# Top-32 attention and an ELU feed-forward on one core: the last queries of two batches as a block of their own, and two query tiles taken one by one

## The chip, the cores and the metric

The kernel runs on one core of a Trainium2 chip. A core has five engines that work side by side, each on its own queue of instructions in a fixed order: TensorE (PE, matrix products and transposes), VectorE (DVE), ScalarE (ACT), GpSimd (POOL) and SyncE (SP, which issues transfers). They wait for each other through semaphores. The metric is the device time of one execution in microseconds (us); the time before is the median of three runs, 1645.8 us (1644.03 to 1645.95).

## The reference

Eight batches of eight heads, 576 queries and keys of 64 numbers each; then a feed-forward of width 2048 over the 4608 tokens of 512 numbers. The weights arrive as 64-bit floats, all arithmetic of the kernel is fp32.

```python
scores = scale * np.matmul(q, k.transpose(0, 1, 3, 2))
kth = np.partition(scores, -top_k, axis=-1)[..., -top_k:-top_k + 1]   # top_k = 32
scores = np.where(scores >= kth, scores, -1000000000.0)
attn = np.exp(scores - np.max(scores, axis=-1, keepdims=True))
attn = attn / (np.sum(attn, axis=-1, keepdims=True) + 1e-09)
attn_out = np.matmul(attn, v)
x = attn_out.transpose(0, 2, 1, 3).reshape(B * S, H * D)              # 4608 x 512
h = x @ w_in                                                          # 512 x 2048
g = np.where(h > 0.0, h, np.exp(np.minimum(h, 0.0)) - 1.0)
out = g @ w_out                                                       # 2048 x 512
```

## The kernel before

**Attention.** The queries of a batch are cut into four tiles of 128 (qt 0 to 3) and a rest of 64 (qt 4, called J). A `Step` is one query tile with one pair of heads (`hp`), or the rest with four heads; a batch has 4 x 4 + 2 = 18 steps, and the program 144. In a step PE computes the scores (`scores`, L331, out tile scps) and ACT copies them out (L339); DVE finds the 32 largest of each row with MAX8 and MATCH_REPLACE8 (`select`, L373 to L385); ACT masks and exponentiates (`mask`, L407, L408); POOL normalises (`normalise`, L418 to L425); PE transposes the probabilities (`turn`, L444, eps) and ACT copies them to et (L445). When all tiles of a `Group` have been turned, PE multiplies with v (`attend`, L470, avps), for all its tiles at once, and ACT writes the result to the transposed input xT of a block (`finish`, L497).

**Order.** From step `tight` = 8 on, the order of every engine is the order in which the program is written. Program step n issues the scores of step n+2, the attend of the groups that are complete, DVE's selection for step n, the mask of step n-1, and the transposes of step n-2. The steps of an even batch run through the tiles (0, 1), (2, 3), J, those of an odd batch through J, (0, 1), (2, 3); within a pair of tiles the two alternate, head pair by head pair, and share a group. Only in batch 0 the four tiles go one by one. The k and q of later batches are loaded some steps ahead by SP and transposed by DVE (`transpose_qk`, L285, kqT); there are five kqT buffers for the four head pairs of a batch.

**Feed-forward.** Queries that go through the feed-forward together are a `Block`, of one to three slots of 128 tokens. Batches are planned in twos: the list `division` (L605, L607) names the tiles of each block, 0 to 3 for the even batch, 4 to 7 for the odd one, and `rest` for one slot that holds the 64 last queries of both. When all tiles of a block are there, `finish` appends the block's pieces to a list `ffn`: 16 pieces `hidden(f)`, each four products into hps (L545) with 128 columns to a slot, the ELU on ACT (L555 to L564) and its last sum, a "gate", on POOL (L515), or on DVE (L517) early and for the last block; then for each slot four pieces `project`, each four products into ops (L573) with 512 columns. Pieces are taken from the front of the list only. An fp32 product is two instructions on PE.

**Pace.** The function `feed` is called four times in a step and takes pieces while a running allowance holds. Every piece has a planned cost: HIDDEN[slots] for a hidden piece, PROJECT for a project piece (L21, L22), in planned us. Every block has a place `ready`, in steps, at which it will be complete; `due` lists it with the sum of the costs of all blocks ahead of it. The allowance grows by the smallest, over the blocks still to come, of the work ahead of the block divided by the steps left until it is ready. What is left after the last step is issued at the end without pause (`while ffn`).

T (L104) is the number of tokens of the widest block; it sizes the tiles of xT, gT and n. A block of one slot takes its xT from a pool of three (`xpool`), a wider one from a pool of two. The weights are decoded from 64-bit floats in the first steps (L176 to L193); pieces wait until their weights are there (`decoded`).

Of the kernel before, what the change touches and what calls it, by code (L numbers as in the profile page):

```python
# [17 lines left out]
TAKEN = -1.0e30  # L18
EPS = 1.0e-9
STEEP = 2.0**96  # L20
HIDDEN = {1: 1.1, 2: 1.85, 3: 2.7}  # L21
PROJECT = 3.55  # L22


# [57 lines left out]
def kernel(  # L82
# [10 lines left out]
    P = nc.NUM_PARTITIONS  # L93
# [7 lines left out]
    NC = dm // P  # L101
    NF = dff // P
    NG = NF // 2
    T = 3 * P  # L104
    KEYS, QUERIES = R, R + S
    Q = 32
    NB = S // Q
# [383 lines left out]
    def finish(blk, parts, at, cols, src):  # L491
        if blk.xT is None:
            if blk.slots == 1:
                blk.xT = xpool.tile([P, NC, P], FP32, tag="xT", name="xT")
            else:
                blk.xT = late["x"].tile([P, NC, T], FP32, tag="xT", name="xT")
        nc.scalar.copy(blk.xT[:, at, cols], src)  # L497
# [23 lines left out]
    def ffn_pieces(blk):  # L521
# [4 lines left out]
        def hidden(f):  # L526
# [3 lines left out]
            elif f % NG == 0 and blk.number > 0:  # L530
                g = late["g"].tile([P, NG, T], FP32, tag="g", name="gT")
                blk.gT.append(g[:])
            if f % unit == 0:
# [4 lines left out]
                else:  # L538
                    n = late["f"].tile([P, 2 * T], FP32, tag="n", name="n")
                blk.n = n[:, 0 : unit * n_tok].rearrange("p (f t) -> p f t", f=unit)  # L540
# [45 lines left out]

        part = HIDDEN[blk.slots]
        behind = 2 * NF if blk.number else 0
# [13 lines left out]
    for b in range(B):  # L602
        if b % 2 == 0:
            rest = 2 * J
            division = [(0,), (1,), (2,), (3,), (rest,), (4, 5), (6, 7)]  # L605
            if b > 0:
                division = [(0, 1), (2, 3), (rest, 4, 5), (6, 7)]  # L607
            slots = {}
            for part in division:
                blk = Block(len(blocks), len(part))  # L610
                blocks.append(blk)
                slots.update((x, (blk, s)) for s, x in enumerate(part))
        first[b] = len(steps)
        tiles = []
        for qt in range(J + 1):
            r0 = b * S + (JP if qt == J else qt if b == 0 else qt * P)
            if qt == J:
                (blk, slot), c0, n = slots[rest], (b % 2) * R, R
                rows = slice(r0, r0 + R)
            else:  # L620
                (blk, slot), c0, n = slots[(b % 2) * J + qt], 0, P
                rows = slice(r0, r0 + J * (P - 1) + 1, J) if b == 0 else slice(r0, r0 + P)
            c0 += slot * P
            t = Tile(b, qt, rows, blk, slice(c0, c0 + n))
            blk.left += NHP
            blk.tiles[slot].append(t)
            tiles.append(t)
        order = [(0, 1), (2, 3), (J,)] if b % 2 == 0 else [(J,), (0, 1), (2, 3)]
        if b == 0:
            order[:2] = [(0,), (1,), (2,), (3,)]  # L630
        for qts in order:
            for hp in range(NHP // 2 if qts == (J,) else NHP):
                group = Group([tiles[qt] for qt in qts], hp)
                steps += [Step(tiles[qt], hp, group, i) for i, qt in enumerate(qts)]
            for qt in qts:
                n = len(steps)
                tiles[qt].block.ready = n + 1.0 if n <= tight else n + 2.5
    NS = len(steps)
    total = 0.0
    for blk in sorted(blocks, key=lambda x: x.ready):  # L640
        due.append((blk.ready, total))
        total += NF * HIDDEN[blk.slots] + 4 * blk.slots * PROJECT

# [57 lines left out]
    main, rest, other = slice(0, J), slice(J, J + 1), slice(J + 1, 2 * J + 1)  # L701
# [90 lines left out]
```

## Time and profile before

| | |
|---|---|
| median of three runs | 1645.8 us |
| the profiled execution | 1642.57 us, its span 1640.8 us |
| busy: PE, DVE, ACT, POOL | 1581.7, 1453.4, 1187.7, 708.7 us |
| hps products, L545 | 1408 instructions of 256 columns, 640 of 128, 384 of 384 |
| ops products, L573 | 1152 instructions of 512 columns |
| avps products, L470 | 1120 of 256 columns, 320 of 128, 640 of 64 |
| DVE's selection, L373 to L385 | 136 steps of 8 MAX8 and 6 MATCH_REPLACE8, about 0.75 us each |
| last selection of DVE ends at | 1520 us |

An instruction of PE starts before the one ahead of it has ended, and the ends in the profile are modelled. So the price of a group of matmuls is best read from start to start: from the start of the first to the start of what follows. A step of DVE is read from one L373 to the next but one (a step has two, shown as one line where they follow each other). The granted clock of PE is 0.5 to 0.9 of full speed in the first 164 us, and 0.98 to 1.00 after.

### The profile page before, as it was taken

The page shows a single profiled execution, that of the slowest core. Times are in us where ns is not written, and L with a number is a line of the kernel's source. Part 1 is how long each engine was busy: PE and PEld are TensorE (multiplying, and loading weights), DVE is VectorE, ACT ScalarE, POOL GpSimd, SP SyncE. Part 2 cuts the span into 40 slices and gives each one's busy share as a digit, 9 for nine tenths or more (in the row PEclk, how much of TensorE's full clock was granted, in tenths as well). Part 3 has the DMA queues.
Part 4 walks back from the last instruction along what each step waited for, and adds up shares of the span by engine and source line. Part 5 has one row for each costly group of instructions (what it writes and reads, how often), then busy time and mean ns, then how long its engine had stood idle before and what let it go on. Part 6 is the DMA issues. An engine that isn't in the chain of part 4 may idle for free.

```text
span 1640.8 us, 25344 instructions
## 1 busy us (share of the span) xinstructions
PE 1581.7 (96%) x8276; PEld 1011.8 (62%) x8276; DVE 1453.4 (89%) x2981; ACT 1187.7 (72%) x2400; POOL 708.7 (43%) x1534
## 2 busy tenths in 40 slices
PE   4788999999999999999999999999999999999999
PEld 3566777666575757555566666655557575755564
DVE  6987999999999999999999699999999599998000
ACT  6887778778695867778678686868759595958521
POOL 4775445445353534445335353535435353534300
PEclk8579999999999999999999999999999999999999
DMA  7431221012100310012100211012100201000000
GB/s 226 151 128 25 50 40 26 7 22 45 42 1 7 59 42 8 7 22 44 36 14 15 43 30 28 1 28 44 36 14 0 43 1 35 1 13 2 7 13 14
DMA packets 188037, 56.18 MB, mean 34 GB/s; under 512 B 178177, under 2 KB 179201, under 8 KB 187905
## 3 DMA queue, kind: packets, MB, share of 16 engines
q1 hardware_dynamic: 186704, 54.26, 14.1%
q8 instruction: 66, 1.08, 0.3%
q14 instruction: 67, 0.54, 0.1%
q10 hardware_dynamic: 1200, 0.30, 0.1%
HBM read 45.09 MB, written 9.44 MB: 33 GB/s over the span
## 4 chain that ended last, share of the span: by engine, by line
PE 76%; ACT 12%; DVE 7%; POOL 3%; issue 1%; DMA 1%; SPq 0%; ACTq 0%; DVEq 0%; POOLq 0%
PE ops L573 29%; PE hps L545 23%; PE avps L470 10%; PE scps L331 7%; PE eps L444 6%; DVE wk L378 3%; DVE m L385 3%; ACT sc L408 2%; ACT et L445 2%; ACT sc L407 2%; DVE m L373 1%; ACT n L564 1%; ACT n L555 1%; ACT sc L339 1%; ACT n L560 1%
## 5 line engine op out<-in xcount | busy, mean ns | idle before, releaser
L385 DVE MAX8 m<-wk 128x8 f32<-128x576 f32 x816 | 577.9, 752 | 0.3 <-POOL den L406 0.3
L545 PE MATMUL hps<-xT,w_in 128*128 128x256 f32 (+2 forms) x2432 | 545.8, 374 | 0.0
L573 PE MATMUL ops<-w_out,gT 128*128 128x512 f32 x1152 | 523.6, 599 | 0.0
L545 PEld LDWEIGHTS hps<-xT,w_in 128*128 128x128 f32 x2432 | 406.0, 192 | 100.1 <-issue 26.3
L378 DVE MATCH_REPLACE8 wk<-m,wk 128x576 f32<-128x576 f32 x544 | 401.4, 748 | 0.0
L573 PEld LDWEIGHTS ops<-w_out,gT 128*128 128x128 f32 x1152 | 209.0, 190 | 233.9 <-issue 232.8
L418 POOL TENSOR_SCALAR dene<-den 128x2 f32<-128x2 f32 x144 | 32.9, 228 | 686.5 <-ACT sc L408 686.1
L408 ACT ACTIVATE sc<-sc,den 128x576 f32<-128x576 f32 x288 | 223.6, 776 | 65.5 <-POOL den L406 44.2
L407 ACT ACTIVATE sc<-sc,m 128x576 f32<-128x576 f32 x288 | 225.3, 782 | 10.8 <-DVE m L385 10.7
L470 PE MATMUL avps<-et,vT 128*64 128x256 f32 (+2 forms) x2080 | 207.2, 330 | 17.4 <-ACT et L445 17.2
L425 POOL TENSOR_SCALAR sc<-sc,rec 128x576 f32<-128x576 f32 x288 | 213.0, 750 | 15.0 <-POOL rec L423 0.2
L331 PE MATMUL scps<-kqT 64*128 64x288 f32 (+1 forms) x1280 | 206.0, 442 | 13.6 <-ACT kqT L307 9.1
L339 ACT ACTIVATE sc<-scps 128x576 f32<-128x576 f32 x288 | 171.8, 647 | 65.1 <-PE scps L331 65.1
L445 ACT COPY et<-eps 128x512 f32<-128x512 f32 x288 | 164.6, 571 | 73.4 <-PE eps L444 73.4
L378 DVE MATCH_REPLACE8 wk<-m,sc 128x576 f32<-128x576 f32 x272 | 200.6, 748 | 0.0
L373 DVE MAX8 m<-sc 128x8 f32<-128x576 f32 x272 | 191.6, 749 | 8.8 <-ACT sc L339 8.8
L444 PEld LDWEIGHTS eps<-ident,sc 128*128 128x128 f32 x1152 | 144.9, 144 | 87.2 <-issue 52.7
L444 PE MATMUL eps<-ident,sc 128*128 128x128 f32 x1152 | 177.1, 279 | 13.7 <-POOL sc L425 13.7
L470 PEld LDWEIGHTS avps<-et,vT 128*64 128x64 f32 x2080 | 128.5, 142 | 98.8 <-ACT et L445 31.7
L515 POOL TENSOR_TENSOR gT<-n,gT 128x512 f32<-128x512 f32 (+1 forms) x119 | 164.9, 1386 | 31.2 <-ACT n L564 31.1
L331 PEld LDWEIGHTS scps<-kqT 64*128 64x128 f32 (+1 forms) x1280 | 111.3, 182 | 89.5 <-issue 43.8
L555 ACT ACTIVATE n<-hps 128x512 f32<-128x512 f32 (+1 forms) x156 | 87.3, 559 | 56.8 <-PE hps L545 56.0
(53 smaller groups left out, 1089.6 us busy)
## 6 DMA issues: line engine op xcount, KB each, us to landing
raw<-in_moe_w_in_dram SPq DMA_DIRECT2D x16, 512.0 KB, 6.1
vT<-in_v_dram SPq DMA_DIRECT2D x64, 128.0 KB, 2.5
raw<-in_moe_w_out_dram SPq DMA_DIRECT2D x16, 512.0 KB, 3.6
out_dram<-osb SPq DMA_DIRECT2D x32, 256.0 KB, 2.1
kin<-in_k_dram SPq DMA_DIRECT2D x112, 72.0 KB, 2.5
qin<-in_q_dram SPq DMA_DIRECT2D x112, 72.0 KB, 2.6
kin<-in_k_dram SPq DMA_DIRECT2D x8, 128.0 KB, 4.5
vT<-in_v_dram SPq DMA_DIRECT2D x64, 16.0 KB, 2.2
```

Source lines behind the costliest of these rows:

```text
L331: nc.tensor.matmul(wide[i][rows, half, 0:HS], kq[part, q0 : q0 + u.t.ql], kq[part, k0 : k0 + HS], start=True, stop=True,)
L373: nc.vector.max(found[i], cur[i])
L378: nc.vector.match_replace(wk[i], found[i], cur[i], TAKEN)
L385: nc.vector.max(found[i], cur[i])
L407: nc.scalar.activation(sc, sc, AF.Prelu, scale=-1.0, bias=low, alpha=1.0 / STEEP)
L408: nc.scalar.activation(sc, sc, AF.Exp, scale=-STEEP, bias=gap, accum_out=u.den[:, i : i + 1])
L425: nc.gpsimd.tensor_scalar(u.sc[:, i, :], u.sc[:, i, :], rec[:, i : i + 1], 1.0, ALU.mult, ALU.mult)
L444: nc.tensor.transpose(ps[:, c * P : (c + 1) * P], sc[:, c0 : c0 + P], ident[:])
L445: nc.scalar.copy(g.et[:, chunks, u.at, :], ps[:, 0 : n * P].rearrange("p (c q) -> p c q", c=n),)
L470: nc.tensor.matmul(ps[i * D : (i + 1) * D, cols], vt[:, 2 * J + i if c == J else i * J + c, :], w, start=(c == 0), stop=(c == J),)
L545: nc.tensor.matmul(blk.h[:, f % bank, :], w_in[:, i, f * P : (f + 1) * P], blk.xT[:, i, 0:n_tok], start=(i == 0), stop=(i == NC - 1),)
L573: nc.tensor.matmul(blk.o[:], blk.gT[f // NG][:, f % NG, s * P : (s + 1) * P], w_out[:, f, :], start=(f == 0), stop=(f == NF - 1),)
```

## The change

The first two batches' block (4, 5) becomes two blocks, (4,) and (5,), and in batch 1 the tiles 0 and 1 (4 and 5 of the pair of batches) are taken one after the other, each with groups of its own. In the later pairs of batches the block of rest, 4, 5 becomes a block of the rest alone and a block (4, 5). No block has three slots any more; T shrinks to two slots, and the planned cost of a three-slot piece goes.

```diff
-HIDDEN = {1: 1.1, 2: 1.85, 3: 2.7}
+HIDDEN = {1: 1.1, 2: 1.85}
...
-    T = 3 * P
+    T = 2 * P
...
-            division = [(0,), (1,), (2,), (3,), (rest,), (4, 5), (6, 7)]
+            division = [(0,), (1,), (2,), (3,), (rest,), (4,), (5,), (6, 7)]
             if b > 0:
-                division = [(0, 1), (2, 3), (rest, 4, 5), (6, 7)]
+                division = [(0, 1), (2, 3), (rest,), (4, 5), (6, 7)]
...
             order[:2] = [(0,), (1,), (2,), (3,)]
+        if b == 1:
+            order[1:2] = [(0,), (1,)]
```

## The prediction

> **What bounds the kernel now.** I read the page first, then PE's timeline in three places, DVE's, the waits, and PE's order in the changed program. The page's first lines and slices:
>
> ```profile
> span 1640.8 us, 25344 instructions
> PE 1581.7 (96%) x8276; PEld 1011.8 (62%) x8276; DVE 1453.4 (89%) x2981; ACT 1187.7 (72%) x2400; POOL 708.7 (43%) x1534
> ...
> PE   4788999999999999999999999999999999999999
> ...
> DVE  6987999999999999999999699999999599998000
> ```
>
> Two engines are nearly full until slice 37; then PE works on alone. PE's busy time is modelled, so I take prices from starts. The first three lines below are early, the next five from 1119 us on, the last two end the program:
>
> ```profile
> 205.64 1.06 PE L545 MATMUL hps<-xT,w_in 128*128 128x128 f32 x8
> 206.53 0.60 PE L444 MATMUL eps<-ident,sc 128*128 128x128 f32 x4
> ...
> 411.07 3.60 PE L573 MATMUL ops<-w_out,gT 128*128 128x512 f32 x8
> ...
> 1118.92 2.75 PE L545 MATMUL hps<-xT,w_in 128*128 128x384 f32 x8
> ...
> 1128.58 0.60 PE L444 MATMUL eps<-ident,sc 128*128 128x128 f32 x4
> 1129.11 1.24 PE L331 MATMUL scps<-kqT 64*128 64x288 f32 x8
> 1130.28 0.65 PE L470 MATMUL avps<-et,vT 128*64 128x256 f32 x2
> 1131.68 2.37 PE L470 MATMUL avps<-et,vT 128*64 128x256 f32 x18 [0.76 <-ACT et L445]
> ...
> 1581.64 27.79 PE L545 MATMUL hps<-xT,w_in 128*128 128x256 f32 x128
> 1609.27 27.63 PE L573 MATMUL ops<-w_out,gT 128*128 128x512 f32 x64
> ```
>
> Eight hps matmuls of 128 columns take 206.53-205.64 = 0.89 us, 0.111 each. At 256 columns it is (1609.27-1581.64)/128 = 0.216, at 512 (ops) 27.63/64, about 0.43, at 384 I take 0.322 (eight run 2.58 us start to start). The price goes with the columns; 128 is only 4% dearer per column than 256. One fp32 product is two instructions in the trace. Attention costs PE 1.17 (scores) + 0.98 (nine transposes) + half of 2.31 (avps of two tiles) = 3.3 us a step.
>
> DVE's pace:
>
> ```profile
> 629.08 1.42 DVE L373 MAX8 m<-sc 128x8 f32<-128x576 f32 x2
> ...
> 638.71 1.42 DVE L373 MAX8 m<-sc 128x8 f32<-128x576 f32 x2
> ```
>
> A step costs DVE 9.64 us, 10.96 where a k and q pair is transposed. Now the waits:
>
> ```profile
> DVE kqT L285 <- PE scps L331: 32.3, 3, 16.9
> ```
>
> DVE loses 32 us in three places to PE's scores, not the other way round: in steps 86 and 122 PE lies 14 and 17 us behind DVE, and DVE stops till PE has caught up. So late in the kernel PE binds. Earlier it leads: it issues the scores that open step 28 at 321.3 us, when DVE starts step 28 at 329.3.
>
> From the starts of PE's scores groups I cut its time into four stretches. Work is instructions times the prices above, gap the rest:
>
> - steps 12 to 35, 170.5 to 407.0: 236.5 us, feed-forward 136.5, attention 79.4, gap 20.6 (0.86 a step)
> - steps 36 to 71, to 774.5: 367.5, feed-forward 224.6, attention 119.6, gap 23.3 (0.65 a step)
> - steps 72 to 140, to 1507.1: 732.7, feed-forward 480.1, attention 230.5, gap 22.1 (0.32 a step)
> - the end, to 1640.8: 133.7, feed-forward 114.3, attention 13.0, gap 6.4
>
> No step has a gap much below 0.2, the price of changing between kinds of matmul. The first two stretches hold some 28 us above that, where feed() rations pieces so that they last until the next block is ready. The last 55 us are the last block, which nothing can precede.
>
> **What the change does to PE's work.** In units of the planner a block of one tile costs 16 x 1.1 + 4 x 3.55 = 31.8, of two 58.0, of three 85.8. Before, the block of rest,4,5 in the second pair is ready at place 66.5 and only 391 units lie ahead of it; at step 12, with 44 done, that allows 347/54.5 = 6.4 a step, and the block (4, 5) of the first pair at 30.5 allows 6.2. After, 428 units lie ahead of 66.5 with 47 done: 7.0 a step; the tightest is 6.6 (place 38.5), then 7.1 to 7.2. After the heavy block's turn the old rate jumps to 10.7 for eight steps; that jump goes.
>
> PE's instruction order in the changed program shows this without the planner. Feed-forward work issued ahead of the scores of step 14 is 40.4 us against 37.7 (+2.7); of step 38, 180.0 against 174.2 (+5.9); of step 74, 423.3 against 398.8 (+24.5: hps 512 of 128 columns and 256 of 256, ops 232; before 320, 256, 60 of 384, and 208); of step 143, 901.1 against 878.9 (+22.2). What is left behind the last scores falls from 114.3 to 94.7.
>
> *More work.* hps products go from 320/704/192 (128/256/384 columns) to 640/832/0: 320 x 0.222 + 128 x 0.432 - 192 x 0.645 = +2.5 us. The four head pairs of the split tiles do 20 avps matmuls of 256 columns (2.31) as two of 128 (1.24 each): +0.7. Sum +3.2.
>
> The kernel's own table puts a narrow piece at 1.1 for 8 instructions, 0.137 each, which would be 640 x 0.026 = 17 us more; the trace's 0.111 stands against it. The Trainium skill ("TensorE: Matmul & The Clock Gate", section "Back-to-back issue gap") speaks against narrow pieces too: in a stream of weight loads and matmuls it gives about 81 ns at 128 columns where the isolated gap would be 56. An estimate from it, 640 further narrow instructions at 25 ns, is +16 us in place of +2.5; the row of eight in 0.89 us decides against it.
>
> *Steps 8 to 11.* Step 10 gets 2.7 us more hps. DVE closes one gate more there (0.7 us) and waits for each group in its queue, with the next MATCH_REPLACE8 behind it; it already waits 5.7 us at that place. I let everything after start 2.7 later. Bounds: 0, if DVE's wait covers it, and 5.
>
> *Steps 12 to 35.* DVE sets the pace and PE leads. PE's work grows by 3.2 + 0.7 = 3.9 in a gap of 20.6: +0. If the cover fails, +3.9; a gain is excluded, since DVE does not stop there except in step 14.
>
> *Steps 36 to 71.* DVE needs 768.0-410.4 = 357.6 us. PE's work becomes 344.2 + 18.7 = 362.9, more than DVE's: PE binds, and the waits for DVE's results go. I take the gap of the stretch that is already so, 0.32 a step: 11.5. So 374.4 against 367.5: +6.9. Ends: gap of 0.2 a step (+2.6); the whole old gap of 23.3 stays (+18.7).
>
> *Steps 72 to 140.* Work -2.4. Waits of PE in the 384 column steps (104, 106, 107, 108, 140) stand some 4.5 us above the others; such a piece fills a PSUM buffer alone, and there are two. -2.4 - 4.5 = -6.9. Ends: -10.7 (0.2 a step), -2.4 (waits remain). DVE will stop earlier and more often, in steps 50 or 86; that costs nothing while PE binds.
>
> *The end.* 114.3 - 94.7 = -19.7. The last block could start when its queries are attended. DVE finishes at 1520 now; PE would come to the last block near 1563, so DVE may be late by some 28 us, less the chain of mask, normalise, transposes and avps of about 15, before this gain shrinks.
>
> *At nothing.* ACT: 48 pairs of 0.485 and 24 pairs of 0.845 become 36 times 0.592 + 0.593 + 0.633 and 35 of 0.630: 87 us both ways, beside 28% idle. POOL: 24 gates of 1.82 become 35 of 1.28, both 44 us, at 43% busy. SP: as many output DMAs, some moved ahead of k and q loads; those wait for osb, up to the 17 us that PE lags, while the loads are issued one to two steps before use. No wait of DVE on a load shows in the steady steps before; if one came it would stop DVE, not PE, by a few us. Smaller tiles (T) change no count of buffers, and single blocks use xpool's three.
>
> **Sum**, on the profiled execution of 1642.57 us (span 1640.8): +2.7 + 0 + 6.9 - 6.9 - 19.7 = -17.0. That execution lies 3.2 below the median of the three runs, 1645.8. I forecast 1645.8 - 17 = 1629 for the median. 0.2%, 3.3 us, is about what this measurement can tell from no change.
>
> **Rivals.** (1) *PE is packed to the change-over price.* With 0.2 a step: 0 + 0 + 2.6 - 10.7 - 19.7 = -27.8, 1618. For it: steps 74 to 81 do run at 0.21. Against: every eighth step or so waits 0.5 more for ACT even there. (2) *The waits are not slack (slower).* Place: steps 12 to 71, PE waiting for ACT's et copies. If these are round trips that each step pays whatever PE has to do, the whole gap stays: 2.7 + 3.9 + 18.7 - 2.4 - 19.7 = +3.2, 1649; 64 further pieces, each paying a change-over of 0.1, make it 1655. It decides from the point where less than 3 of the 28 us go. For it: a 0.76 us wait for et stands in a step where PE lags. Against: 0.32 a step where PE lags and 0.65 to 0.86 where it leads. (3) *Half of it.* In steps 36 to 71 half the gap stays: +5.9, with the 384 column waits replaced by others (+4.5): 1640. (4) *No effect*, pieces held back as before: excluded by the order.
>
> **How the numbers follow.** Forecast 0.55, own range 1622 to 1636; rival 1 0.14; rival 3 0.18; rival 2 0.13, of which 0.04 ends within 0.2%. Range 1618 to 1642 leaves out most of rival 2 and the far side of rival 1. Faster 0.83 (rival 3 loses 0.03 to "same"), same 0.07, slower 0.10.
>
> **What would show it.** Right: PE issues the last scores within some 5 us of 1507 and works about 114 us after; PE leads DVE no more past step 50; DVE's wait for scores appears in step 50 or grows beyond 32 us in total; hps of 128 columns at 0.111 a piece in the later pairs. Wrong: gaps of 0.65 a step or more after step 36, the last scores later than 1520, a new DVE wait for k or q loads, or narrow pieces at 0.13 and above.

## The result: slower by 1.0%, and the profile after

The changed kernel takes 1661.4 us (median; 1660.27 to 1664.39) beside 1645.1 us for the kernel before on the same chip. The ratio is 1.0102, with a 95% interval of 1.0085 to 1.012. The forecast was 1629 us, so its sign was wrong. The profiled execution took 1660.88 us, its span 1659.1 us; all comparisons of parts below are made between spans.

The first lines and slices of the page of the changed kernel:

```profile
span 1659.1 us, 26574 instructions
PE 1580.8 (95%) x8868; PEld 1059.1 (64%) x8868; DVE 1453.3 (88%) x2982; ACT 1190.9 (72%) x2403; POOL 711.4 (43%) x1545
...
PE   5788999999999999999999999999999999999999
...
DVE  6978999999999899999989599999999779999400
```

PE's busy time is what it was (1581.7 before), yet the span is 18.3 us longer. The slices show nothing of it: PE still reads 9 everywhere. A wait of 1 to 2 us in a step of 10 is too short for them. The waits show more (columns: total us, times, longest). These three lines are the changed kernel's. In the kernel before, the same waits were 31.7 us in 40 places (PEld, the weight loads), 32.3 us in 3 (DVE for scores) and 17.2 us in 21 (PE at avps):

```profile
PEld avps L470 <- ACT et L445: 51.2, 36, 3.4
...
DVE kqT L285 <- PE scps L331: 43.1, 4, 18.4
...
PE avps L470 <- ACT et L445: 36.9, 31, 2.7
```

PE waits for ACT's copy of the probabilities to et before avps, 19.7 us more than before. DVE's wait for PE's scores appears in a fourth place, step 50, as the forecast said it would.

Where the time came from, with PE cut into the same four stretches as in the forecast (length, and in brackets the gap left over the instructions at their prices):

| stretch | before | forecast | after | after against forecast |
|---|---|---|---|---|
| start to step 12 | 170.5 | 173.2 | 169.8 | -3.4 |
| steps 12 to 35 | 236.5 (20.6) | 236.5 | 236.3 (16.5) | -0.2 |
| steps 36 to 71 | 367.5 (23.3) | 374.4 (11.5) | 383.6 (20.7) | +9.2 |
| steps 72 to 140 | 732.7 (22.1) | 725.8 (17.6) | 751.4 (43.2) | +25.6 |
| the end | 133.7 (6.4) | 114.0 | 118.1 | +4.1 |

The saving at the end came: 15.6 us of the 19.7. But steps 72 to 140 lost 18.7 us where 6.9 were to be won, although PE had 2.4 us less to do in them.

One such step, in PE's timeline of the changed kernel (start, duration, what; in brackets the idle time before and what ended it):

```profile
832.91 1.24 PE L331 MATMUL scps<-kqT 64*128 64x288 f32 x8
834.08 0.65 PE L470 MATMUL avps<-et,vT 128*64 128x256 f32 x2
835.69 2.37 PE L470 MATMUL avps<-et,vT 128*64 128x256 f32 x18 [0.97 <-ACT et L445]
838.00 3.72 PE L545 MATMUL hps<-xT,w_in 128*128 128x256 f32 x16
```

The 18 later avps matmuls begin 1.61 us after the first two. At 0.116 us a piece, the two should take 0.23, so the step loses some 1.4 us. In ACT's timeline of the same moment:

```profile
832.83 0.19 ACT L408 ACTIVATION_READ_ACCUMULATOR sc<-sc,den 128x1 f32 x1
832.92 0.58 ACT L555 ACTIVATE n<-hps 128x512 f32<-128x512 f32 x1
833.40 0.59 ACT L558 ACTIVATE gT<-hps 128x512 f32<-128x512 f32 x1
833.88 0.63 ACT L560 ACTIVATE n<-n 128x512 f32<-128x512 f32 x1
834.54 0.63 ACT L564 ACTIVATE n<-n 128x512 f32<-128x512 f32 x1
835.08 0.57 ACT L445 COPY et<-eps 128x512 f32<-128x512 f32 x1
```

The copy that PE waits for starts at 835.08. Four operations of the feed-forward's ELU, from 832.92 to 835.08, stand ahead of it. In the same kind of step of the kernel before, PE's timeline and then ACT's read:

```profile
1045.92 1.24 PE L331 MATMUL scps<-kqT 64*128 64x288 f32 x8
1047.09 2.92 PE L470 MATMUL avps<-et,vT 128*64 128x256 f32 x20
```

```profile
1046.93 0.19 ACT L408 ACTIVATION_READ_ACCUMULATOR sc<-sc,den 128x1 f32 x1
1047.02 0.56 ACT L445 COPY et<-eps 128x512 f32<-128x512 f32 x1
1047.48 0.60 ACT L555 ACTIVATE n<-hps 128x512 f32<-128x512 f32 x1
```

Here the copy follows ACT's mask at once, the ELU comes after it, and the 20 avps matmuls run without a break.

### The profile page after: what moved, and what is told of

It is laid out like the page before. It is cut to its first block, busy times and chain, and to the rows that moved or that the text cites. A ratio compares the mean times of both kernels' runs of the same rounds, so it can differ in the third digit from the quotient of the medians.

```text
span 1659.1 us, 26574 instructions
## 1 busy us (share of the span) xinstructions
PE 1580.8 (95%) x8868; PEld 1059.1 (64%) x8868; DVE 1453.3 (88%) x2982; ACT 1190.9 (72%) x2403; POOL 711.4 (43%) x1545
## 4 chain that ended last, share of the span: by engine, by line
PE 68%; ACT 25%; POOL 3%; issue 2%; DMA 1%; SPq 0%; DVE 0%; ACTq 0%; POOLq 0%
PE ops L573 29%; PE hps L545 17%; PE avps L470 10%; PE scps L331 7%; ACT sc L408 5%; PE eps L444 5%; ACT sc L407 4%; ACT et L445 3%; ACT n L564 3%; ACT n L555 3%; ACT n L560 3%; ACT gT L558 2%; ACT sc L339 1%; DMA raw<-in_moe_w_out_dram 1%; POOL sc L425 1%
## 5 line engine op out<-in xcount | busy, mean ns | idle before, releaser
L385 DVE MAX8 m<-wk 128x8 f32<-128x576 f32 x816 | 619.7, 855 | 3.0 <-POOL den L406 3.0
L545 PE MATMUL hps<-xT,w_in 128*128 128x256 f32 (+1 forms) x2944 | 551.5, 339 | 0.0
L545 PEld LDWEIGHTS hps<-xT,w_in 128*128 128x128 f32 x2944 | 458.2, 193 | 61.6 <-issue 22.6
L378 DVE MATCH_REPLACE8 wk<-m,wk 128x576 f32<-128x576 f32 x544 | 429.1, 851 | 0.0
L470 PE MATMUL avps<-et,vT 128*64 128x256 f32 (+2 forms) x2160 | 205.9, 322 | 37.0 <-ACT et L445 36.9
L373 DVE MAX8 m<-sc 128x8 f32<-128x576 f32 x272 | 205.4, 849 | 27.4 <-ACT sc L339 27.3
L515 POOL TENSOR_TENSOR gT<-n,gT 128x512 f32<-128x512 f32 x130 | 166.1, 1278 | 121.9 <-ACT n L564 121.9
L378 DVE MATCH_REPLACE8 wk<-m,sc 128x576 f32<-128x576 f32 x272 | 213.9, 846 | 0.0
L555 ACT ACTIVATE n<-hps 128x512 f32<-128x512 f32 x144 | 85.0, 590 | 77.0 <-PE hps L545 76.9
```

The costliest lines, as they stand in the source:

```text
L373: nc.vector.max(found[i], cur[i])
L378: nc.vector.match_replace(wk[i], found[i], cur[i], TAKEN)
L385: nc.vector.max(found[i], cur[i])
L470: nc.tensor.matmul(ps[i * D : (i + 1) * D, cols], vt[:, 2 * J + i if c == J else i * J + c, :], w, start=(c == 0), stop=(c == J),)
L545: nc.tensor.matmul(blk.h[:, f % bank, :], w_in[:, i, f * P : (f + 1) * P], blk.xT[:, i, 0:n_tok], start=(i == 0), stop=(i == NC - 1),)
```

## The theory and its rivals

**Theory: ACT's order.** A pair of hidden pieces of a two-slot block (or four pieces of a one-slot block) fills one tile n. Its last piece is called the closing piece here: when it is issued, ACT gets L555, L558, L560 and L564. A program step has four calls of `feed`; the third (L748) stands just ahead of `turn(done, other)` (L750), whose copy of the last probabilities is the last one that the attend at the opening of the next step needs. PE issues that attend directly behind 1.17 us of scores. If the third feed issues a closing piece, 2.2 us of ELU (832.92 to 835.08 above) lie between the mask and that copy, and PE stands still. If it issues the opening piece of a two-slot block, or none, nothing lies between them. Two shorter cases remain: any hidden piece of a three-slot block brings L555 and L558 (6 more steps from 12 to 140 of the kernel before), and the last project piece of a slot brings the copy L582 (5 steps after).

ACT's order is fixed by the program, so such steps can be counted. I call a step *blocked* if all four operations stand directly ahead of its last et copy. In steps 12 to 35, 36 to 71 and 72 to 140 there are 4, 8 and 2 before, and 5, 8 and 29 after. Both kernels share the pattern of two pieces, one, one in a step's feeds, but after the change it is shifted by one piece: the single piece of the third feed is now the closing one. One late two-slot block of the changed kernel, in steps 126 to 129, kept the old phase: no step of it is blocked, and the steps have gaps of 0.2 us, where the two steps with an attend behind blocked steps of the block before it, 120 and 122, have 1.8 and 2.4.

**Rival A: PE cannot be packed denser.** Rival 2 of the prediction: the round trips of each step cost PE their time whatever it has to do, and 64 more pieces cost change-overs. Then moving ACT's operations changes little.

**Rival B: the narrow pieces are dear.** 128 columns cost more in the later pairs than the early row showed.

**Rival C: the first pair's part**, with its single tiles and groups of their own, delays what follows.

In the recorded expectations the theory is called P and rival B is called N. Rival L there is one more: PE waits because it lies 16 to 21 us behind DVE, whatever ACT's order.

## Experiments

All are timed against the kernel before on their chip: 1642.19 us for the first four, 1643.31 for the next four, 1643.16 for the last three. In the fourth column are the blocked steps by stretch, in the fifth the gaps by stretch, in the sixth PE's waits within avps over the whole program, from start to start. Of these, 15.3 us before, 35.5 after and 2.6 in e1 lie in steps 12 to 140. The four groups of runs differ by up to 3 us in the kernel before, so small differences between kernels of different groups are better taken from the ratios.

| kernel | us | ratio (95%) | blocked | gap, us | avps waits, us |
|---|---|---|---|---|---|
| before | 1645.1 | 1 | 4 / 8 / 2 | 20.6 / 23.3 / 22.1 | 25.0 |
| after | 1661.4 | 1.0102 (1.0085 to 1.012) | 5 / 8 / 29 | 16.5 / 20.7 / 43.2 | 46.2 |
| e1 after, hold | 1616.2 | 0.984 (0.9825 to 0.9855) | 0 / 0 / 0 | 12.0 / 13.0 / 15.7 | 8.0 |
| e2 before, force | 1717.7 | 1.046 (1.0445 to 1.0476) | 11 / 21 / 31 | 30.6 / 40.0 / 67.9 | 75.0 |
| e3 after, copy first | 1619.4 | 0.9862 (0.9847 to 0.9877) | 0 / 0 / 0 | 12.0 / 14.8 / 15.6 | 9.4 |
| e4 before, copy first | 1635.4 | 0.995 (0.9933 to 0.9967) | 0 / 0 / 0 | 18.2 / 21.7 / 19.6 | 16.3 |
| e5 first pair only | 1644.3 | 1.0009 (1.0 to 1.0019) | 4 / 9 / 2 | 17.9 / 27.2 / 23.1 | 28.8 |
| e6 later pairs only | 1667.5 | 1.0143 (1.0125 to 1.0161) | 6 / 13 / 29 | 22.4 / 20.9 / 42.9 | 50.5 |
| e7 before, hold | 1634.9 | 0.9947 (0.9932 to 0.9963) | 0 / 0 / 0 | 20.4 / 19.8 / 19.8 | 19.2 |
| e8 after, attend late | 1623.9 | 0.9883 (0.9867 to 0.9899) | 5 / 8 / 29 | 12.1 / 14.1 / 19.0 | 8.3 |
| e9 after, hold from 72 | 1628.6 | 0.9914 (0.9899 to 0.9929) | 5 / 8 / 0 | 16.5 / 20.5 / 16.0 | 19.3 |
| e10 after, hold, attend late | 1621.1 | 0.9865 (0.985 to 0.988) | 0 / 0 / 0 | 12.1 / 12.5 / 18.9 | 7.6 |
| e11 later pairs, hold | 1617.6 | 0.9851 (0.9825 to 0.9876) | 0 / 0 / 0 | 17.3 / 8.5 / 16.2 | 12.3 |

### e1: the changed kernel, the third feed issues no closing piece

Every piece carries a mark that says whether it is a closing one. The third feed stops ahead of such a piece; the fourth feed of the same step, behind the copy, may take it. Blocks, pieces, their order and what is planned stay.

```diff
-            (part, max(behind, NC * (f // 4 + 1)), lambda f=f: hidden(f))
+            (part, max(behind, NC * (f // 4 + 1)), lambda f=f: hidden(f), (f + 1) % unit == 0)
...
-             lambda s=s, part=part: project(s, part))
+             lambda s=s, part=part: project(s, part), False)
...
-    def feed(n, share):
+    def feed(n, share, third=False):
...
-            cost, _, piece = ffn.pop(0)
+            if third and ffn[0][3]:
+                break
+            cost, _, piece, _ = ffn.pop(0)
...
         next(passes)
-        feed(n, 0.25)
+        feed(n, 0.25, True)
         if done:
             turn(done, other)
```

> The changed kernel, but the third feed of a step never issues a hidden piece that closes a gate unit (the piece after which ACT has four feed-forward instructions to do). PE's feed-forward work by step is as in the changed kernel (423 us ahead of step 74's scores, 901 ahead of the last). Theory P (phase): the changed kernel is slow because in 28 of 69 late steps these four instructions of ACT, 2.4 us, stand directly ahead of the last et copy, and PE's first avps of the next step waits for it (46 us of such waits in the changed kernel against 25 before, 22 against 2 in steps 72 to 140). Here no step has them there: avps waits fall below 20 us in all and the time falls by 18 to 28, to 1634 to 1643. Rival L (lag): PE waits because it lies 16 to 21 us behind DVE, and ACT's queue is then out of step whatever its order: 1655 to 1665, waits as in the changed kernel. Rival N (narrow): the pieces of 128 columns cost more than 0.111 us an instruction: 1655 to 1665.

Measured: 1616.2 us, 45 us less than the changed kernel (42 if each is counted from the kernel before on its own chip) and 1.6% less than the kernel before. The theory's direction holds, its size was too small: the time is 18 us below the lower end expected. In steps 72 to 140 the gap goes from 43.2 to 15.7, and the stretches 12 to 35 and 36 to 71, which had blocked steps in the kernel before as well, become 4.5 and 7.8 us shorter. PE's timeline of one step of e1, and ACT's beside it:

```profile
822.15 1.24 PE L331 MATMUL scps<-kqT 64*128 64x288 f32 x8
823.32 2.38 PE L470 MATMUL avps<-et,vT 128*64 128x256 f32 x20
825.63 3.72 PE L545 MATMUL hps<-xT,w_in 128*128 128x256 f32 x16
```

```profile
822.07 0.19 ACT L408 ACTIVATION_READ_ACCUMULATOR sc<-sc,den 128x1 f32 x1
822.16 0.56 ACT L445 COPY et<-eps 128x512 f32<-128x512 f32 x1
822.62 0.60 ACT L555 ACTIVATE n<-hps 128x512 f32<-128x512 f32 x1
```

The copy is done 0.6 us before PE comes to avps; the 20 matmuls take 2.31 us from start to start. From scores to hidden pieces it is 3.48 us, where the step at 832.91 above needed 5.09: 1.6 us a step. e1's waits:

```profile
DVE kqT L285 <- PE scps L331: 34.8, 3, 16.8
...
PEld avps L470 <- ACT et L445: 9.7, 12, 3.4
...
PE avps L470 <- ACT et L445: 5.3, 8, 2.5
```

PE's waits at avps fall from 36.9 to 5.3 us. Rival A falls: the same pieces in the same blocks do fit. Rival L falls with it: DVE still waits 34.8 us for PE's scores, so PE still lags.

### e2: the kernel before, the closing piece forced into the third feed

The reverse, on the old blocks: where a closing piece is next, the third feed takes it, allowance or not, and books it as ever. With the marks of e1:

```diff
-    def feed(n, share):
+    def feed(n, share, third=False):
...
+        while third and ffn and ffn[0][3] and decoded[0] >= ffn[0][1]:
+            cost, _, piece, _ = ffn.pop(0)
+            fed["over"] -= cost
+            fed["sum"] += cost
+            piece()
```

> The kernel before, but the third feed always goes on to issue the hidden piece that closes a gate unit, when that is the next. Blocks, pace and PE's work stay (399 us ahead of step 74's scores, 881 ahead of the last). Theory P: 63 steps from 12 to 140 instead of 14 have ACT's four instructions ahead of the last et copy, 31 of them from step 72 on, where PE binds; those cost some 0.8 us each (half of them have no attend behind them): slower by 12 to 25, 1657 to 1670. Rival L and rival N: nothing of theirs is touched, 1642 to 1650.

Measured: 1717.7 us, 4.6% slower, far above what was expected. The order alone, with the work of the kernel before, makes a loss. A second wait came with it that I had not counted, in PE's timeline of this kernel:

```profile
1087.32 0.75 PE L331 MATMUL scps<-kqT 64*128 64x288 f32 x2
1089.88 1.23 PE L331 MATMUL scps<-kqT 64*128 64x288 f32 x6 [1.81 <-ACT et L445]
1091.04 0.65 PE L470 MATMUL avps<-et,vT 128*64 128x256 f32 x2
1091.98 2.37 PE L470 MATMUL avps<-et,vT 128*64 128x256 f32 x18 [0.29 <-ACT et L445]
```

The last six scores matmuls wait 1.81 us for an et copy too. In steps 72 to 140 the gap is 67.9, where the changed kernel, with two blocked steps less, has 43.2. The granted clock has a part in it. In this kernel's trace it falls to 0.50 in ten stretches after 168 us, 37.4 us in all, each beside a wait of PE for et of 1.9 to 2.7 us (not every such wait has one); at 1317.01 the 18 avps matmuls behind such a wait take 3.66 us in place of 2.31. The kernel before has one such stretch (3.4 us), the changed kernel two (6.8), e1 none. Half of 37.4, some 19 us, is an estimate of the most that this adds to e2's loss of 75.

### e3 and e4: the copy ahead of the third feed

`turn(done, other)` goes ahead of the third feed, so that nothing the feed issues can stand before the copy; e3 on the changed kernel, e4 on the one before. No piece is held back.

```diff
         next(passes)
-        feed(n, 0.25)
         if done:
             turn(done, other)
+        feed(n, 0.25)
         next(passes)
```

> The changed kernel with the second half of the transposes (the last et copy with it) ahead of the third feed instead of behind it. Theory P: as with the held piece, no step has the four instructions ahead of the last et copy, and it also comes some 2 us earlier in every step: 1625 to 1640. Rival L: 1655 to 1665. A third reading, that the transposes need the feed as cover for ACT's mask (mask of the second head pair stands ahead of the copy): PE waits for POOL or et at the transposes instead, 1650 to 1670.

Measured: 1619.4 us, 5.6 below the lower end expected. A second way of keeping the ELU off that copy gives nearly the same time and the same gap (15.6) in steps 72 to 140 as e1.

> The kernel before with the same move of the transposes ahead of the third feed. Theory P: the 25 us of avps waits lie mostly in steps 12 to 71, where DVE sets the pace, so little comes of it: 1635 to 1644. If the changed blocks are worth what their earlier work promises, the changed kernel with the move is 8 to 17 us faster than this one; if not, the two are within 5.

Measured: 1635.4 us. The kernel before wins 0.5% by it. With the copy clear in both, the change itself is worth 1619.4 - 1635.4 = -16.0 us.

### e5 and e6: each half of the change

e5 keeps the old division for the later pairs:

```diff
-HIDDEN = {1: 1.1, 2: 1.85}
+HIDDEN = {1: 1.1, 2: 1.85, 3: 2.7}
...
-    T = 2 * P
+    T = 3 * P
...
-                division = [(0, 1), (2, 3), (rest,), (4, 5), (6, 7)]
+                division = [(0, 1), (2, 3), (rest, 4, 5), (6, 7)]
```

> Only the part of the first two batches: blocks (4,) and (5,) and the two tiles of batch 1 one by one; the later pairs keep the block of rest, 4, 5. In its order ACT's four feed-forward instructions stand ahead of the last et copy in 15 steps, 2 of them from step 72 on, as in the kernel before (14 and 2). Theory P: close to before, at most 6 us faster (6 us of feed-forward work pulled ahead): 1634 to 1643. Rival (the split of the first pair costs, through narrow pieces or its additional avps matmuls): 1645 to 1655.

Measured: 1644.3 us, ratio 1.0009 (1.0 to 1.0019): no change, just above the range expected. Steps 12 to 35 became 2.4 us shorter and 36 to 71 4.2 us longer. Two blocked steps in 72 to 140, as before, and no loss there. Rival C falls.

e6 keeps the old division and order of the first pair:

```diff
-            division = [(0,), (1,), (2,), (3,), (rest,), (4,), (5,), (6, 7)]
+            division = [(0,), (1,), (2,), (3,), (rest,), (4, 5), (6, 7)]
...
-        if b == 1:
-            order[1:2] = [(0,), (1,)]
```

> Only the part of the later pairs: a block of the rest alone and a block (4, 5); the first two batches as before. The order has the four instructions ahead of the last et copy in 48 steps, 29 of them from step 72 on, as in the changed kernel. Theory P: the loss is here: 1650 to 1670. Rival: if the loss came from the first pair, 1625 to 1640.

Measured: 1667.5 us, as expected. The 29 blocked steps and the gap of 42.9 come with the later pairs' division. Beside it the first pair's part saves 5.5 us in steps 12 to 35 (241.8 against 236.3); by itself it saved half of that, and nothing in the total.

### e7: the kernel before with e1's hold

The edit of e1 on the kernel before.

> The kernel before with the third feed holding back a closing piece, as in the first experiment. Theory P: little is to be had from step 72 on, and DVE sets the pace before that: 1630 to 1640, that is 14 to 24 us above the changed kernel with the same edit (1616), which is then what the change of blocks is worth by itself; my forecast said 17. If the blocks are worth nothing by themselves: 1612 to 1620.

Measured: 1634.9 us, as expected. With the hold in both kernels the change is worth 1616.2 - 1634.9 = -18.7 us (-17.6 if each is counted from the kernel before on its own chip). This kernel still has 19.2 us of avps waits, 0.6 of them past step 72. Some 8 lie in steps 12 to 140, where no step is blocked, the rest ahead of step 12; what these early ones stand behind was not followed up.

### e8: the changed kernel, the attend behind the first feed

The pieces stay where they are and the blocked steps stay 29. Only PE's attend moves behind the first feed, so that its own pieces give ACT time:

```diff
-        while closing:
-            attend(closing.pop(0))
         next(passes)
         feed(n, 0.25)
+        while closing:
+            attend(closing.pop(0))
```

> The changed kernel with the four instructions left where they are, but the attend of a complete group placed behind the first feed of a step instead of ahead of it, so that PE has feed-forward matmuls (some 3.5 us) to do while the last et copy waits. If the time is lost by PE standing at avps, most of it comes back: 1617 to 1635. If it is ACT's order that costs by another way (the next step's scores or masks coming late): 1650 to 1665.

Measured: 1623.9 us, as expected. This separates the order on ACT from what waits for it: the ELU still stands ahead of the copy, in as many steps, and costs almost nothing more, since PE has other work at that moment. Its waits at avps are 5.8 us in 4 places, against 36.9 in 31.

### e9: the hold from step 72 on only

e1 with `if third and n >= 72 and ffn[0][3]:`.

> The changed kernel with closing pieces held back by the third feed from step 72 on only; 13 steps before that keep ACT's four instructions ahead of the last et copy. Held everywhere it was 45 us faster than the changed kernel, whose avps waits are 22 us from step 72 on and 13 in steps 12 to 71. If the late stretch alone is what the forecast missed, 27 us come back (its gap of 43.2 falls to 16 to 18): 1630 to 1638; if the early steps matter as much, 1640 to 1650.

Measured: 1628.6 us, a little below what was expected. From step 12 to 72 both lengths are within 0.2 us of the changed kernel's; steps 72 to 140 fall from 751.4 to 724.2. That is 27.2 us for 29 blocked steps, 0.94 us each on average, but the average hides where it is lost. An attend opens only some of the steps that follow a blocked one. In the changed kernel 16 such steps with an attend hold 30.8 us of the gap, where e9 has 3.9 in the same steps: 1.7 us each, all but 0.3 us of the difference. The 12 without an attend hold 3.2, and 3.1 in e9. So a blocked step costs where PE comes to avps next, and nothing elsewhere, as the theory says. What e1 gains beyond e9, some 12 us (4.4 and 7.6 in the two stretches ahead of step 72), is the blocked steps there.

### e10 and e11: both cures, and the later pairs alone with the hold

e10 is e1 with e8's move, e11 is e6 with e1's hold.

> Both cures on the changed kernel: the third feed holds closing pieces back, and the attend stands behind the first feed. The wait is one and the same, so the second cure should find little: 8 us of avps waits are left, most of them early. 1608 to 1617. If the two add up (45 and 38 us), far below 1600, the reading of one wait is wrong.

Measured: 1621.1 us, above the range expected and above e1. The cures do not add up, and once no ELU stands ahead of the copy the later attend costs a little: the gap in steps 72 to 140 is 18.9 with it and 15.7 without. e8 has the same 19.0, so the late attend itself carries some 3 us there. Why, I did not settle.

> Only the later pairs' part of the change, with closing pieces held back. With the first part it was 1616. The first part alone made no difference, and pulls 6 us of feed-forward work ahead of step 38: 1616 to 1624.

Measured: 1617.6 us, as expected, and the same as e1 within its interval. With the hold, the division of the later pairs alone is all that is needed; the first two batches' part makes no difference that these runs can tell.

## Why the prediction was wrong

**The step that failed** is "*Steps 72 to 140*": its term of -6.9 measured +18.7. "Work -2.4" is not in question, since e1, with the same instructions, has a stretch of 723.9 us where 725.8 were forecast. "Waits of PE in the 384 column steps ... stand some 4.5 us above the others" went with the wide pieces: e1's gap is 15.7, where 17.6 was forecast. What failed is the end of the range: gap terms from 0.2 to 0.32 a step were the only ones considered, that is, the waits that remain were taken over from the old order. 27 more blocked steps brought (43.2 - 17.6) = 25.6 us over the forecast, and e9 takes 27.2 us away by treating these steps alone.

The root is the entry "*At nothing.* ACT: ... 87 us both ways, beside 28% idle". It compares amounts. ACT's queue is in order, and an ELU that is as long as before can stand ahead of a copy that PE needs, or behind it. ACT has 28% idle in both kernels and still makes PE wait in one of them. A line of my own fence showed it: the 0.76 us before the avps matmuls at 1131.68. In ACT's timeline of the kernel before, just ahead of the copy that ends that wait, stand the two operations of an ELU:

```profile
1130.31 0.47 ACT L555 ACTIVATE n<-hps 128x384 f32<-128x384 f32 x1
1130.68 0.48 ACT L558 ACTIVATE gT<-hps 128x384 f32<-128x384 f32 x1
1131.05 0.58 ACT L445 COPY et<-eps 128x512 f32<-128x512 f32 x1
```

I listed such waits as belonging to the wide pieces, "such a piece fills a PSUM buffer alone", and let them go with them. In this step, the wait followed from what the ELU stood in front of.

**"*Steps 36 to 71*", +6.9, measured +16.1.** PE binds there, as said, and DVE's wait in step 50 shows it. But "the waits for DVE's results go" did not cover avps: PE waits there 7.7 us in 6 places (7.4 in 8 before). With the hold the gap is 13.0, forecast 11.5, and the stretch 375.8, forecast 374.4.

**"*The end*", -19.7, measured -15.6.** The last block starts without a wait, so the selections that were feared to be late were not. In this stretch too a blocked step waits, in PE's timeline of the changed kernel:

```profile
1550.27 0.65 PE L470 MATMUL avps<-et,vT 128*64 128x256 f32 x2
1553.62 3.33 PE L470 MATMUL avps<-et,vT 128*64 128x256 f32 x18 [2.71 <-ACT et L445]
...
1600.01 27.79 PE L545 MATMUL hps<-xT,w_in 128*128 128x256 f32 x128
1627.63 27.63 PE L573 MATMUL ops<-w_out,gT 128*128 128x512 f32 x64
```

The 2.71 us and the slower 18 matmuls after it (3.26 us to the next start, where the 18 at 835.69 take 2.31) are 3.7 of the 4.1 missing. These matmuls are slower since the granted clock is lower there: 0.50 from 1555 to 1557, behind that wait, and 1.00 again from 1560. The last block itself runs as before. With the hold the stretch is 112.4, forecast 114.0.

**"*Steps 8 to 11*", +2.7, measured -0.8.** The lower bound, 0, was the nearer end: the additional pieces delayed nothing. **"*Steps 12 to 35*", 0, measured -0.2**, right in size. But there was something to win: e1 and e3, without blocked steps, and e8, whose blocked steps hold up nothing, take 231.8, although "a gain is excluded, since DVE does not stop there". With the first pair's part, these steps depend on PE after all; without it, e7 and e11 stay at 236.3 and 236.6 although no step is blocked.

**The price of narrow pieces held.** In the changed kernel's later pairs 16 instructions of 128 columns run from 1104.29 to the transposes at 1106.08, 0.112 us each:

```profile
1104.29 1.95 PE L545 MATMUL hps<-xT,w_in 128*128 128x128 f32 x16
1106.08 0.60 PE L444 MATMUL eps<-ident,sc 128*128 128x128 f32 x4
```

This rules out rival B. (Against the 0.216 at 256 columns, 0.111 is about 3% dearer per column, not the 4% of the prediction.) The Trainium skill ("TensorE: Matmul & The Clock Gate", section "Back-to-back issue gap") gives about 81 ns at 128 columns in a stream, against an isolated gap of 56. The prediction's estimate from it, +16 us, happens to be the size of the loss measured; but these rows and e1, which has all the narrow pieces and is 25.6 us shorter in span than the kernel before, decide against it here.

**Rival 2** of the prediction had the right wait, "PE waiting for ACT's et copies", and the wrong place and reason. It looked for it in steps 12 to 71, as a round trip that each step pays; in fact what was added came in steps 72 to 140, in those steps only where a closing piece stood ahead. So it priced it at +3.2, and what it named as decisive, "where less than 3 of the 28 us go", was not what decided. (Rival 3's terms add up to 1639, not 1640.)

Without blocked steps, the forecast's own sum was about right: it said -17.0, and the change brings -18.7 with the hold in both kernels and -16.0 with the copy first in both. Part of that agreement is luck. Stretch by stretch, e3 less e4 is -1.2, -2.3, +11.7, -6.3 and -18.5, where the forecast had +2.7, 0, +6.9, -6.9 and -19.7: the two late terms were nearly right, and the errors of the three early ones cancel. The worth of the blocks came out right; the effect of a shift by one piece on ACT's order, not looked at, was larger than it.

What shifted the pattern by one piece is argued only: the allowance of the planner passes its threshold at another of the four feeds, since the costs 1.85 and 1.1 and the blocks' due places differ from those with 2.7. e5 and e6 show that it comes with the later pairs' division. Other planned costs, which would shift the pattern without changing the blocks, were not tried.

## What to carry to other kernels

When a change shifts pieces of filler work against a fixed cycle, read the order on every in-order engine that the pieces feed, not only the amounts: for each copy that the bounding engine waits for, list what stands directly ahead of it, before and after. Here that list stands in the program's order (2 such places against 29 in the late steps), and a rule that keeps a long operation from the place ahead of such a copy was worth more (42 to 45 us) than the new blocks themselves (16 to 19 us).

## What the runs showed that was not expected

A loss of 1 to 2.5 us in every fifth step or so is nearly invisible in shares. In the changed kernel 26 of 129 steps open with an attend behind a blocked step; they hold 48.9 us of the gap, and 7.6 in e1. Yet PE is 95% busy in the changed kernel at 1661 us and 97% in e1 at 1616 us. Part of it is recorded as busy: the pair of avps matmuls that opens the group, at 834.08, has 0.65 us on record and 1.61 to the next start, and only 0.97 is called a wait.

In the profiled execution of the changed kernel, DVE's recorded durations wander while its pace does not. DVE's timeline at two moments:

```profile
500.30 1.74 DVE L385 MAX8 m<-wk 128x8 f32<-128x576 f32 x2
503.07 1.74 DVE L385 MAX8 m<-wk 128x8 f32<-128x576 f32 x2
...
899.37 1.42 DVE L385 MAX8 m<-wk 128x8 f32<-128x576 f32 x2
902.14 1.42 DVE L385 MAX8 m<-wk 128x8 f32<-128x576 f32 x2
```

The pair of MAX8 is on record with 1.74 and with 1.42 us, but it is 2.77 us to the next in both. Over the program the mean of these instructions is 855 ns here and 752 in the kernel before; in the other runs it is 742 to 759. So a comparison of mean durations would have blamed DVE. The cause stays open.
